# Softmax of three half blocks summed by ScalarE, and a new order of issue, in an attention and feed-forward kernel on one core

## The chip, the cores and the metric

The kernel runs on one core of a Trainium2 chip. The time is the device time of one execution in microseconds (us). Before the change three runs took 591.66, 591.89 and 592.00 us, with a median of 591.89 us. The core has five engines that work beside each other and wait for each other by semaphores: TensorE (PE, matrix products), VectorE (DVE), ScalarE (ACT), GpSimd (POOL) and SyncE (SP, which issues all loads and stores here).

## The reference

The reference computes chunked attention and feeds it to a two-layer network with a gate between the layers:

```python
for c in range(nc):                       # 24 chunks of 32 queries
    k_full = concat([mem_k, k[c_start-16 : c_end+8]])   # 8 + 56 keys
    scores = scale * q_c @ k_full.T       # scale = 1 / sqrt(64)
    scores = scores - max(scores)
    a = exp(scores)
    a = a / (sum(a) + 1e-09)
    out[c] = a @ v_full
h = x @ w_in                              # x: 3072 x 512, w_in: 512 x 2048
g = where(h >= 1, h, where(h <= -1, 0, (h + 1)**2 / 4))
return g @ w_out                          # w_out: 2048 x 512
```

There are 4 batches, 8 heads, 768 positions and 64 numbers a head. All inputs and the output are float32; the two weight matrices come in as 64-bit words.

## The kernel before

**Blocks and halves.** The 3072 tokens are cut into six blocks of 512, and each block into two halves of 256. For a half block PE makes the scores (tile `ps_s`, two PSUM banks of 128 x 1024 numbers in all: 16 groups of 64 keys on 128 partitions), the softmax turns them into probabilities (`pr`), DVE transposes these in 32 x 32 squares (`pt`), PE multiplies them with the values (`ps_x`), and the result is split into a rounded part and a residual (`xth`, `xtl`) for the layers. The first block goes another way: its heads come in four parts (`first_attention`), and PE transposes the probabilities.

**Banks.** The scores and the value products of every half block lie in the same two banks (tag `s`). The next one can't be written before the last reader of the one ahead is done with them. Parts three and four of the first block lie in another pair (tag `a1`).

**Layers.** The hidden width of 2048 is cut into 16 slices. For a slice and a block, PE makes a hidden product of 12 matmuls (rounded weight by rounded x, residual weight by rounded x, rounded weight by residual x; tile `ps_h`), ACT and DVE make the gate (two ACT instructions into `gw`, one DVE minimum, one ACT rounding into `gh`, one DVE residual into `gl`), and PE makes 12 output matmuls (`ps_o`). Products over half a block have 128x256 instead of 128x512 hidden matmuls.

**Weights.** Each pair of weight slices is loaded once and decoded (`decode`): one ACT instruction, two DVE instructions into `f`, one ACT rounding into `wr`, one DVE residual into `wr`.

**Softmax before.** DVE takes the maximum of each group of 64 (`mx`), DVE writes scores less maximum to `pr`, ACT takes the exponent of all 128x1024 in one instruction, DVE sums (`den`), and `divide` adds 1e-9, takes the reciprocal and multiplies. One part of the first block (`SUMMED = (2,)`) already goes another way: there ACT reads the scores' bank group by group, and each instruction gives a group's exponents and its sum.

**Order.** Every engine runs its instructions in the order in which the program issues them (`InOrder`). For the first two blocks and the attention of the third, that order is a table, `FIRST` (line 32): each name in it advances one chain by one step. `L0` to `L39` start a load; `g0` to `g3` are the four parts of the first block's attention; `n0`, `n1` are the two halves of the second block, `n2`, `n3` those of the third; `u0` to `u3` and `w2` to `w15` decode weights; `A`, `B` and `J` are slices of the first block's layers (first half, second half, whole block), and `C`, `D`, `E` those of the second block. `J14` is slice 14 of the first block over the whole block. The last four blocks are issued by the loop at line 662, which isn't touched. The diff's parts stand in `decode` (line 157), `less_max` (338) and `attention` (453); `divide` (211) is called by both ways of the softmax.

Of the kernel before, what the change touches and what calls it, by code (L numbers as in the profile page):

```python
# [29 lines left out]


FIRST = """
    L0 L1 L5 g0 L2 L3 u0 L9 L8 g0 g0 L6 g0 g0 u0 g1 g2 g0 u0 u0 L10 g0 g1 g1 g0 g0 g1 u1 g1 L12 g1
    L7 g1 L4 L13 L11 g1 u2 g0 g1 g2 g1 L14 u2 u0 g0 g1 u2 u1 g2 g3 L16 u1 L15 g2 g0 g2 u2 g2 g3 g1
    L30 u3 u1 L18 g1 g3 g0 L17 u1 L19 g0 g0 g2 g3 g3 g3 A0 g2 A1 g3 g3 A0 A0 u2 g3 w2 g3 g2 A1 L26
    L21 u3 L25 L27 L20 g3 u3 u3 w2 A2 g3 w2 A1 A0 g3 L22 A1 g2 u3 w2 n0 g2 w2 A0 B0 n0 A1 A0 A2 B0
    w3 w4 A1 A2 n0 B0 w3 A3 w4 B1 w3 A2 A3 L28 B0 A3 B0 L23 L31 B0 B2 L24 B1 w3 B1 w4 A2 w3 n0 w5 w5
    L32 L29 B2 B3 B2 B1 B3 A3 A2 n0 n0 B3 A3 w5 w7 w4 B2 J4 B1 B3 J4 n0 w4 B2 n0 n0 J4 B1 J4 n0 w7
    n0 B2 J5 A3 w5 w5 n0 w13 w6 w8 w7 J6 w6 B3 w6 J5 J4 J5 B3 w6 w6 n0 J4 J6 w12 n0 J5 w8 J5 w7 w10  # L39
    J7 J5 w7 J6 w8 J7 w8 w12 J6 n0 w9 w12 w8 J7 n0 w12 J6 J8 J9 J6 J7 J8 w12 n0 w9 J7 w10 w9 n0 J8  # L40
    w9 J8 J9 w11 w9 n1 w10 J9 w11 n1 L33 J10 w10 J7 n1 J8 w10 L34 n1 w11 J10 J10 w15 J10 n1 w13 w14
    J9 J8 J13 n1 w13 J10 n1 J13 J9 J13 n1 n2 J11 w11 J13 w13 J9 J11 w11 J13 w13 J11 n1 w15 n1 J12 n1
    w15 n1 J12 J11 J12 J10 w14 J11 w14 n2 C0 n1 w15 n1 n2 J14 w14 J12 J11 J14 w15 n2 w14 n2 J14 n2
    J12 C0 J14 n1 n2 n2 n2 J12 C0 n2 J15 C1 J14 J15 n1 J13 C1 J15 C0 C0 J15 J15 C1 n1 n1 C2 J14 L36
    J15 n2 C2 C1 L35 J15 n2 J15 n2 n2 C2 J15 C3 C0 C3 C3 C1 n2 C3 n2 D0 D0 D1 D0 C2 D1 D0 J15 D1 D0
    n2 C2 C3 n2 n3 D2 n2 D2 D3 D0 C1 D3 D1 D3 n3 D2 n2 n2 D1 E4 D2 n2 E5 E4 C2 D1 C3 D2 n2 n2 E4 n3
    E4 D3 n3 E4 n3 E5 E5 D3 E5 n3 E7 n3 D2 n3 E5 E7 E7 E6 E8 E6 n3 D3 E4 E7 E5 E6 n3 E6 E6 E9 n3 E8
    n3 E8 E7 E6 E8 E9 n3 n3 E8 E12 L37 E9 E10 E10 E7 E10 E13 n3 E8 E9 L38 L39 E9 E12 E10 n3 E10 E12
    n3 E9 E12 E10 E12 E13 n3 E13 E11 E14 E13 E13 E11 E11 E14 E11 E11 n3 E15 E11 E12 E15 E13 n3 E15
    E14 n3 n3 E14 E15 n3 n3 E14 E15  # L50
"""

LAST = 2
# [1 line left out]

SUMMED = (2,)
HALVED = (0,)
SLICED = (0,1)


class InOrder:
# [13 lines left out]
def attn_ffn_kernel(ctx: ExitStack, tc: tile.TileContext, first_qk, first_v, qk, vw, first_w, w, out):  # L75
    nc = tc.nc
    engines = (nc.tensor, nc.scalar, nc.vector, nc.gpsimd, nc.sync)
    pe, act, dve, pool, sp = (InOrder(tc, e) for e in engines)
# [14 lines left out]
    apool = ctx.enter_context(tc.tile_pool(name="apool", bufs=1))  # L93
# [6 lines left out]
    def two_banks(tag, name):  # L100
        return ps_2.tile([P, 2, 512], F32, name=name, tag=tag)
# [55 lines left out]
    def decode(i, parts=(0, 1)):  # L157

        at = slice(parts[0] * DM, (parts[-1] + 1) * DM)
        pairs = raw[i].rearrange("p (n two) -> p n two", two=2)[:, at]  # L160
        low, u = pairs[:, :, 0], pairs[:, :, 1]
        high = u.bitcast(F32)

        act.activation(high, high, AF.Prelu, scale=2.0**-112, alpha=-(2.0**32))
        yield
        f = apool.tile([P, n2], U32, name="f", bufs=2)[:, at]
        dve.tensor_scalar(f, u, 3, None, op0=ALU.logical_shift_left)
        yield
        dve.scalar_tensor_tensor(f, low, 29, f, op0=ALU.logical_shift_right, op1=ALU.bitwise_or)
        yield  # L170
        f = f.bitcast(F32)
        if i not in ws:
            ws[i] = const.tile([P, 2 * n2], F32R, name=f"wr_{i}", tag=f"w_{i}")
        hi, lo = ws[i][:, 0:n2][:, at], ws[i][:, n2 : 2 * n2][:, at]
        act.copy(hi, f)
        yield
        dve.tensor_tensor(lo, f, hi.bitcast(F32), op=ALU.subtract)
        yield


    scores_of, prob, prob_t, banks, rows_of, turned, xts, both = {}, {}, {}, {}, {}, {}, {}, {}
# [46 lines left out]
    def first_attention(g):  # L228
# [30 lines left out]
        for at in (slice(0, 1), slice(1, 2)) if g in HALVED else (slice(0, 2),):  # L259
# [59 lines left out]
    G = 2 * NP * 2  # L319
# [27 lines left out]
    def transpose_prob(key):

# [104 lines left out]
    def attention(key):  # L453

        pe_scores(key)
        yield
        yield from less_max(key)
        act.activation(prob[key], prob[key], AF.Exp, scale=SCALE)
        yield
        yield from normalise(prob[key])  # L460
        yield from transpose_prob(key)
        if key[0] < first:
            pe_values(key)
            yield
# [12 lines left out]
        yield from split_low(key)
# [184 lines left out]
    for s in range(first * NFC, steps):  # L662
# [5 lines left out]
        if k_values is not None:  # L668
            ps = two_banks("s", "ps_x")
# [28 lines left out]
        else:  # L698
            n, i = LAST // LAG, s - first * NFC
# [22 lines left out]
def _lay_out(q, k, v, mem_k, mem_v, moe_w_in, moe_w_out):  # L722
# [84 lines left out]
```

## Time and profile before

| What | Value |
|---|---|
| Median of three runs | 591.89 us |
| Time of the profiled execution | 591.89 us |
| Span in its profile (first to last instruction) | 590.1 us |
| Granted TensorE clock, mean | 0.998 |
| PE busy | 573.8 us (97%) |
| DVE busy | 338.0 us (57%) |
| ACT busy | 256.9 us (44%) |

The span is 1.8 us shorter than the time. The shares are means over the whole program: DVE is busy 98% in some stretches of the first 110 us, and under a quarter at the end. A matmul's end is modelled, so a busy PE is not always a PE at its full pace; starts of matmuls show the pace.

### The profile page before, as it was taken

Reading aid. Unit: us, or ns where it says so; the run is one execution under the profiler, and the core shown is the slowest. Engines: PE = TensorE matmul, PEld = TensorE weight load, DVE = VectorE, ACT = ScalarE, POOL = GpSimd, SP = SyncE. Lnnn points to the kernel's source line nnn. Section 1 sums busy time; section 2 is a strip of 40 time slices with the busy share of each in tenths; the row PEclk is TensorE's granted clock in tenths of the full one; section 3 lists DMA queues with packets and bytes.
Section 4 is the critical chain, followed back from the end, with each engine's and each line's share of the span. In section 5 each row is a group of like instructions: output and inputs, shape, how many; then the busy total and the mean of one; then the engine's idle time right before and its main releaser. Section 6 shows DMA issues by size and latency. Waiting matters only on the chain.

```text
span 590.1 us, 12015 instructions
## 1 busy us (share of the span) xinstructions
PE 573.8 (97%) x5364; PEld 474.8 (80%) x5364; DVE 338.0 (57%) x497; ACT 256.9 (44%) x430; POOL 2.4 (0%) x7
## 2 busy tenths in 40 slices
PE   4899999999999999999999999999999999999996
PEld 2798888789888888888888888888888888888885
DVE  5899999955643334857624765833684752322222
ACT  3986956344524334343433343333443443433331
POOL 1000000000000000000000000000000000000000
PEclk9999999999999999999999999999999999999999
DMA  8999632205002004103201223201320000100001
GB/s 314 422 418 427 246 111 109 73 37 217 1 1 72 2 0 179 36 38 109 72 1 73 108 72 109 73 1 61 119 72 2 1 1 0 73 1 1 0 1 71
DMA packets 10708, 54.91 MB, mean 93 GB/s; under 512 B 1184, under 2 KB 1184, under 8 KB 6304
## 3 DMA queue, kind: packets, MB, share of 16 engines
q1 hardware_dynamic: 10656, 54.14, 24.1%
q8 instruction: 42, 0.69, 0.5%
q14 instruction: 10, 0.08, 0.0%
HBM read 47.84 MB, written 6.29 MB: 92 GB/s over the span
## 4 chain that ended last, share of the span: by engine, by line
PE 80%; DVE 7%; issue 2%; ACT 2%; DVEq 0%; ACTq 0%
PE ps_o L69 39%; PE ps_h L69 38%; PE ps_x L69 2%; DVE f L69 2%; PE ps_s L69 2%; DVE pt L69 1%; DVE gw L69 1%; DVE gl L69 1%; DVE wr L69 1%; DVE pr L69 0%; DVE den L69 0%; ACT gw L69 0%; DVE mx L69 0%; ACT w L69 0%; ACT wr L69 0%
## 5 line engine op out<-in xcount | busy, mean ns | idle before, releaser
L69 PE MATMUL ps_h<-xth,wr 128*128 128x512 f32 (+1 forms) x832 | 194.5, 376 | 1.1 <-ACT xth L69 1.1
L69 PE MATMUL ps_o<-wr,gh 128*128 128x512 f32 x768 | 194.4, 390 | 0.0
L69 PEld LDWEIGHTS ps_h<-xth,wr 128*128 128x128 f32 x832 | 147.6, 188 | 30.3 <-ACT xth L69 1.3
L69 PEld LDWEIGHTS ps_o<-wr,gh 128*128 128x128 f32 x768 | 143.6, 188 | 29.5
L69 DVE SCALAR_TENSOR_TENSOR gw<-ps_h,gw 128x512 f32<-128x512 f32 (+1 forms) x104 | 67.2, 647 | 140.4 <-ACT gw L69 139.9
L69 ACT ACTIVATE gw<-ps_h 128x512 f32<-128x512 f32 (+1 forms) x104 | 58.5, 563 | 182.5 <-PE ps_h L69 174.1
L69 PE MATMUL ps_o<-wr,gl 128*128 128x512 f32 x384 | 107.1, 390 | 0.5 <-DVE gl L69 0.5
L69 PE MATMUL ps_h<-xtl,wr 128*128 128x512 f32 (+1 forms) x416 | 104.4, 373 | 0.0
L69 DVE TENSOR_TENSOR gl<-gw,gh 128x512 fp32r<-128x512 f32 (+1 forms) x104 | 67.1, 647 | 52.6 <-ACT gh L69 49.9
L69 ACT CAST gh<-gw 128x512 fp32r<-128x512 f32 (+1 forms) x104 | 60.6, 585 | 66.8 <-DVE gw L69 56.6
L69 PEld LDWEIGHTS ps_h<-xtl,wr 128*128 128x128 f32 x416 | 74.9, 188 | 13.9
L69 PEld LDWEIGHTS ps_o<-wr,gl 128*128 128x128 f32 x384 | 71.9, 188 | 16.1 <-DVE gl L69 1.2
L69 ACT ACTIVATE gw<-gw 128x512 f32<-128x512 f32 (+1 forms) x104 | 62.3, 599 | 3.3
L69 DVE STREAM_TRANSPOSE pt<-pr 32x512 f32<-32x512 f32 (+1 forms) x60 | 41.5, 699 | 1.3
L69 DVE STREAM_TRANSPOSE xt<-xr 32x512 f32<-32x512 f32 (+1 forms) x48 | 33.1, 700 | 8.7 <-ACT xr L69 8.0
L69 ACT ACTIVATE pr<-pr 128x1024 f32<-128x1024 f32 (+1 forms) x13 | 12.5, 960 | 30.3 <-DVE pr L69 30.3
L69 PEld LDWEIGHTS ps_s<-qk 64*32 64x32 f32 x1536 | 16.6, 111 | 11.1 <-DMA qk<-in_first_qk_dram 7.2
L69 PE MATMUL ps_s<-qk 64*32 64x64 f32 x1536 | 19.6, 236 | 6.0 <-DMA qk<-in_first_qk_dram 5.1
L69 DVE COPY ob<-ps_o 128x512 f32<-128x512 f32 (+1 forms) x16 | 9.6, 622 | 23.0 <-PE ps_o L69 23.0
L69 ACT ACTIVATE w<-w 128x1024 f32<-128x1024 f32 (+1 forms) x18 | 18.4, 1036 | 6.3 <-DMA w<-in_first_w_dram 6.3
L69 ACT CAST wr<-f 128x1024 fp32r<-128x1024 f32 (+1 forms) x18 | 17.1, 951 | 7.8 <-DVE f L69 7.7
L69 DVE TENSOR_TENSOR wr<-f,wr 128x1024 fp32r<-128x1024 f32 (+1 forms) x18 | 19.7, 1098 | 0.6 <-ACT wr L69 0.5
(36 smaller groups left out, 201.0 us busy)
## 6 DMA issues: line engine op xcount, KB each, us to landing
qk<-in_qk_dram SPq DMA_DIRECT2D x10, 1536.0 KB, 7.1
w<-in_w_dram SPq DMA_DIRECT2D x14, 1024.0 KB, 19.8
v<-in_vw_dram SPq DMA_DIRECT2D x10, 1024.0 KB, 5.0
out_dram<-ob SPq DMA_DIRECT2D x24, 256.0 KB, 2.1
qk<-in_first_qk_dram SPq DMA_DIRECT2D x8, 336.0 KB, 6.9
w<-in_first_w_dram SPq DMA_DIRECT2D x4, 512.0 KB, 8.2
v<-in_first_v_dram SPq DMA_DIRECT2D x4, 512.0 KB, 9.3
```

What stands on the lines that cost most here:

```text
L69: return self.tc.keep_in_program_order(getattr(self.engine, name)(*args, **kwargs))
```

## The change

For the two halves of the second block and the first half of the third, the softmax takes the way of part three of the first block. DVE takes the maximum and multiplies it by minus the scale (a small instruction on 128x16). ACT then reads the scores' banks in 16 instructions on 128x64, each with its group's maximum as bias, and each also gives the sum of its 64 exponents. The subtraction and the sum on DVE fall away for these three, and the exponent in one instruction on ACT. The 16 are issued in four steps of four, so that other work can stand between them. The other halves stay as they were.

`FIRST` is written anew from its first name on. `FLOORED` is empty, so the new branch of `decode` is never taken; `U16` is used only there.

```diff
 FIRST = """
-    L0 L1 L5 g0 L2 L3 u0 L9 L8 g0 g0 L6 g0 g0 u0 g1 g2 g0 u0 u0 L10 g0 g1 g1 g0 g0 g1 u1 g1 L12 g1
...
+    L2 L0 L1 g0 g0 L3 g1 L5 g0 g0 g1 g0 g1 g0 g1 u0 L6 L10 g0 L8 g1 u2 g1 u0 u1 L9 g1 L7 g0 L12 L13
...
-SLICED = (0,1)
+SLICED = (0, 1)
+SUMMED_HALVES = ((1, 0), (1, 1), (2, 0))
+FLOORED = ()
...
-    def less_max(key):
+    def masked(key):
         ps = scores_of.pop(key)
...
         prob[key] = apool.tile([P, G, W], F32, name="pr")
-        yield from softmax_less_max(ps.rearrange("p h (g w) -> p (h g) w", w=W), prob[key])
+        return ps.rearrange("p h (g w) -> p (h g) w", w=W)
+
+    def less_max(key):
+        yield from softmax_less_max(masked(key), prob[key])
+
+    def summed(key):
+
+        s, pr = masked(key), prob[key]
+        mx = apool.tile([P, G], F32, name="mx", bufs=2)
+        dve.tensor_reduce(mx, s, axis=AX.X, op=ALU.max)
+        dve.tensor_scalar_mul(mx, mx, -SCALE)
+        yield
+        den = apool.tile([P, G], F32, name="den", bufs=2)
+        for i in range(G):
+            act.activation(pr[:, i], s[:, i], AF.Exp, bias=mx[:, i : i + 1], scale=SCALE, accum_out=den[:, i : i + 1])
+            if i % 4 == 3:
+                yield
+        yield from divide(pr, den)
...
-        yield from less_max(key)
-        act.activation(prob[key], prob[key], AF.Exp, scale=SCALE)
-        yield
-        yield from normalise(prob[key])
+        if key in SUMMED_HALVES:
+            yield from summed(key)
+        else:
+            yield from less_max(key)
+            act.activation(prob[key], prob[key], AF.Exp, scale=SCALE)
+            yield
+            yield from normalise(prob[key])
```

**The first place: DVE at the start of the program.** `ps_s` are scores of a part of the first block, `pr_...` its probabilities, `w_...` a raw pair of weight slices and `f` its decoded form. Before:

```order
L69 MEMSET ps_s 32x2x2x16
L69 TENSOR_REDUCE mx<-ps_s 128x2x2
L69 TENSOR_TENSOR pr_133<-ps_s,mx 128x2x128
L69 TENSOR_REDUCE mx<-ps_s 128x2x2
L69 TENSOR_TENSOR pr_133<-ps_s,mx 128x2x128
L69 TENSOR_SCALAR f<-w_91 128x512
L69 SCALAR_TENSOR_TENSOR f<-w_91,f 128x512
L69 TENSOR_REDUCE den<-pr_133 128x8
L69 MEMSET ps_s 32x2x2x16
```

With the change:

```order
L72 MEMSET ps_s 32x2x2x16
L72 TENSOR_REDUCE mx<-ps_s 128x2x2
L72 TENSOR_TENSOR pr_126<-ps_s,mx 128x2x128
L72 TENSOR_REDUCE mx<-ps_s 128x2x2
L72 MEMSET ps_s 32x2x2x16
L72 TENSOR_REDUCE mx<-ps_s 128x8
L72 TENSOR_TENSOR pr_126<-ps_s,mx 128x2x128
L72 TENSOR_TENSOR pr_126<-ps_s,mx 128x512
L72 TENSOR_REDUCE den<-pr_126 128x8 x2
```

The second part's softmax moves up into the first's, and the first weights' decoding moves behind both. On SP all four loads for the two parts (`L2 L0 L1 L3`) now stand ahead of the first weights (`L5`), and the load of the second part's first piece stands first.

**The second place: ACT around the exponents of the third block's first half.** `pr` and `den` are its probabilities and sums, the `gw` on 128x512 ahead of them is the gate of `J14`, `wr_1478` is the last but one pair of weights, and `xth` the rounded attention of the second block's second half. Before:

```order
L69 ACTIVATE gw<-ps_h 128x512
L69 ACTIVATE gw<-gw 128x512
L69 ACTIVATE pr<-pr 128x1024
L69 ACTIVATE gw<-ps_h 128x256
L69 ACTIVATE gw<-gw 128x256
```

With the change:

```order
L72 ACTIVATE gw<-ps_h 128x512
L72 ACTIVATE gw<-gw 128x512
L72 ACTIVATE pr,den<-ps_s,mx 128x64 x8
L72 CAST gh<-gw 128x256
L72 CAST wr_1478<-f 128x1024
L72 ACTIVATE pr,den<-ps_s,mx 128x64 x8
L72 CAST gh<-gw 128x512
L72 CAST xth<-ps_x 128x4x2x64 x2
```

One instruction becomes sixteen, with the rounding of a half block's gate and of a pair of weights between them, and the rounding of the attention behind them.

**The third place: PE at the same stretch.** `ps_x` is the value product of the second block's second half, in the banks that held the third block's scores. Before, from the hidden product of `J14` on:

```order
L69 MATMUL ps_h<-xth,wr_1290 128x512 x8
L69 MATMUL ps_h<-xtl,wr_1290 128x512 x4
L69 MATMUL ps_o<-wr_981,gh 128x512 x8
L69 MATMUL ps_o<-wr_981,gl 128x512 x4
L69 MATMUL ps_x<-pt,v 64x32 x64
L69 MATMUL ps_o<-wr_1290,gh 128x512 x8
L69 MATMUL ps_o<-wr_1290,gl 128x512 x4
L69 MATMUL ps_h<-xth,wr_1391 128x512 x8
```

With the change:

```order
L72 MATMUL ps_h<-xth,wr_1361 128x512 x8
L72 MATMUL ps_h<-xtl,wr_1361 128x512 x4
L72 MATMUL ps_h<-xth,wr_205 128x256 x8
L72 MATMUL ps_h<-xtl,wr_205 128x256 x4
L72 MATMUL ps_o<-wr_1121,gh 128x512 x8
L72 MATMUL ps_o<-wr_1121,gl 128x512 x4
L72 MATMUL ps_o<-wr_1361,gh 128x512 x8
L72 MATMUL ps_o<-wr_1361,gl 128x512 x4
L72 MATMUL ps_x<-pt,v 64x32 x64
```

Between the hidden product of `J14` and the value product there was one output product; now there are a half block's hidden product (`C1`) and two output products (`J11`, `J12`).

## Rows read from the trace of the kernel before

**Rows 1.** The page's first lines (the span, and for each engine busy time, share and number of instructions), and the first line of its part on the chain that ended last: shares of the span by engine.

```profile
span 590.1 us, 12015 instructions
PE 573.8 (97%) x5364; PEld 474.8 (80%) x5364; DVE 338.0 (57%) x497; ACT 256.9 (44%) x430; POOL 2.4 (0%) x7
...
PE 80%; DVE 7%; issue 2%; ACT 2%; DVEq 0%; ACTq 0%
```

**Rows 2.** Stretches of the program: start and end, length, busy time of PE, PEld, DVE, ACT and POOL with the number of instructions, granted clock, DMA share, GB/s.

```profile
0.00:10.00 10.00, 4.56 (x132) 2.20 (x132) 3.56 (x9) 2.87 (x4) 2.44 (x7) 1.00 0.78 266
20.00:30.00 10.00, 8.54 (x158) 7.59 (x140) 9.34 (x17) 9.49 (x19) 0.00 (x0) 1.00 1.01 419
...
50.00:60.00 10.00, 10.00 (x45) 8.01 (x44) 9.77 (x13) 6.17 (x8) 0.00 (x0) 1.00 1.03 432
...
100.00:110.00 10.00, 9.98 (x66) 8.24 (x64) 9.81 (x13) 5.79 (x9) 0.00 (x0) 1.00 0.00 0
```

**Rows 3.** PE's waits in the first 220 us: what waited for what, us in total, how often, the longest.

```profile
PE ps_s L69 <- DMA qk<-in_first_qk_dram: 5.1, 4, 2.9
...
PE ps_h L69 <- ACT xth L69: 1.1, 1, 1.1
...
PE ps_o L69 <- DVE gl L69: 0.5, 1, 0.5
```

**Rows 4.** PE in order of time at the start: start us, us, what, how many, and in brackets the idle time ahead and what ended it. The third row is the second part's scores, the fourth the first hidden product (`A0`), the last the scores of the second block.

```profile
3.90 0.68 PE L69 MATMUL ps_s<-qk 64*32 64x64 f32 x32 [0.82 <-DMA qk<-in_first_qk_dram]
4.95 0.68 PE L69 MATMUL ps_s<-qk 64*32 64x64 f32 x32 [0.37 <-DMA qk<-in_first_qk_dram]
8.55 0.68 PE L69 MATMUL ps_s<-qk 64*32 64x64 f32 x32 [2.92 <-DMA qk<-in_first_qk_dram]
...
23.24 1.22 PE L69 MATMUL ps_h<-xth,wr 128*128 128x256 f32 x8 [1.09 <-ACT xth L69]
...
30.94 1.48 PE L69 MATMUL ps_s<-qk 64*32 64x64 f32 x128
```

**Rows 5.** PE in order of time around 114 us, and its last row.

```profile
108.69 1.07 PE L69 MATMUL ps_o<-wr,gl 128*128 128x512 f32 x4
109.77 2.07 PE L69 MATMUL ps_x<-pt,v 64*64 64x32 f32 x128
111.77 2.11 PE L69 MATMUL ps_o<-wr,gh 128*128 128x512 f32 x8
114.40 1.20 PE L69 MATMUL ps_o<-wr,gl 128*128 128x512 f32 x4 [0.51 <-DVE gl L69]
115.43 1.98 PE L69 MATMUL ps_h<-xth,wr 128*128 128x512 f32 x8
...
118.15 1.12 PE L69 MATMUL ps_h<-xth,wr 128*128 128x256 f32 x8
...
119.59 2.00 PE L69 MATMUL ps_o<-wr,gh 128*128 128x512 f32 x8
...
585.21 0.39 PE L69 MATMUL ps_o<-wr,gl 128*128 128x512 f32 x1
```

**Rows 6.** DVE in order of time at the start: the first mask, the two rows with a wait, and the scaling of the third part's maximum.

```profile
5.78 0.11 DVE L69 MEMSET ps_s<- 32x64 f32 x1 [4.64 <-PE ps_s L69]
...
8.40 0.43 DVE L69 TENSOR_SCALAR f<-w 128x512 uint32<-128x512 uint32 x1 [0.80 <-ACT w L69]
...
12.46 0.69 DVE L69 TENSOR_REDUCE den<-pr 128x8 f32<-128x512 f32 x1 [0.38 <-ACT pr L69]
...
15.55 0.17 DVE L69 TENSOR_SCALAR mx<-mx 128x8 f32<-128x8 f32 x1
```

**Rows 7.** Groups of instructions of the whole program by form: engine, operation, out<-in, shapes, how many, busy us in all, mean ns of one, idle time ahead.

```profile
L69 ACT ACTIVATE gw<-gw 128x512 f32<-128x512 f32 x88 | 55.6, 632 | 2.8
...
L69 ACT ACTIVATE gw<-ps_h 128x512 f32<-128x512 f32 x88 | 52.4, 596 | 170.0 <-PE ps_h L69 165.2 <-DVE gl L69 4.7
...
L69 ACT CAST wr<-f 128x1024 fp32r<-128x1024 f32 x14 | 14.7, 1049 | 7.1 <-DVE f L69 7.0
L69 ACT ACTIVATE pr<-pr 128x1024 f32<-128x1024 f32 x10 | 10.6, 1060 | 28.7 <-DVE pr L69 28.7
...
L69 ACT CAST gh<-gw 128x256 fp32r<-128x256 f32 x16 | 6.1, 396 | 2.7 <-DVE gw L69 2.7
...
L69 ACT ACTIVATE pr<-ps_s,mx 128x64 f32<-128x64 f32 x8 | 2.4, 325 | 0.0
...
L69 ACT ACTIVATION_READ_ACCUMULATOR pr<-ps_s,mx 128x1 f32 x8 | 1.7, 218 | 0.0
...
L69 DVE TENSOR_TENSOR pr<-ps_s,mx 128x1024 f32<-128x1024 f32 x10 | 12.2, 1222 | 0.3
L69 DVE TENSOR_REDUCE den<-pr 128x16 f32<-128x1024 f32 x10 | 12.1, 1213 | 0.6 <-ACT pr L69 0.6
```

**Rows 8.** ACT in order of time: the first and second and the end of the eight exponents of part three of the first block, and the rounding that `A0` waits for.

```profile
16.84 0.32 ACT L69 ACTIVATE pr<-ps_s,mx 128x64 f32<-128x64 f32 x1
...
17.15 0.31 ACT L69 ACTIVATE pr<-ps_s,mx 128x64 f32<-128x64 f32 x1
...
19.07 0.24 ACT L69 ACTIVATION_READ_ACCUMULATOR pr<-ps_s,mx 128x1 f32 x1
...
22.60 0.58 ACT L69 CAST xth<-ps_x 128x512 fp32r<-128x512 f32 x1
```

More of the change, by code (lines that the diff above doesn't have):

```diff
@@ L12 @@
 U32 = mybir.dt.uint32
+U16 = mybir.dt.uint16
 AF = mybir.ActivationFunctionType
@@ L32 @@
 FIRST = """
-    L0 L1 L5 g0 L2 L3 u0 L9 L8 g0 g0 L6 g0 g0 u0 g1 g2 g0 u0 u0 L10 g0 g1 g1 g0 g0 g1 u1 g1 L12 g1
[L34 to L47, printed above, removed]
@@ L48 @@
-    n3 E8 E7 E6 E8 E9 n3 n3 E8 E12 L37 E9 E10 E10 E7 E10 E13 n3 E8 E9 L38 L39 E9 E12 E10 n3 E10 E12
-    n3 E9 E12 E10 E12 E13 n3 E13 E11 E14 E13 E13 E11 E11 E14 E11 E11 n3 E15 E11 E12 E15 E13 n3 E15
-    E14 n3 n3 E14 E15 n3 n3 E14 E15
+    L2 L0 L1 g0 g0 L3 g1 L5 g0 g0 g1 g0 g1 g0 g1 u0 L6 L10 g0 L8 g1 u2 g1 u0 u1 L9 g1 L7 g0 L12 L13
+    g1 g1 u0 u0 g0 u2 L4 g0 g2 u2 g0 g1 L16 u2 g2 g1 g2 u0 u2 L14 L15 u1 g2 g3 L11 L30 g2 g0 L20 g1
+    g2 g3 g3 g0 g2 L17 g3 g1 g3 g3 g0 g0 g3 g3 A0 g2 w2 g3 u1 A0 g3 w2 A0 L19 u1 g2 u1 g3 u3 g3 g2
@@ new lines @@
+    A1 A2 w2 u3 g2 g3 L18 u3 L21 A1 n0 w2 A1 u3 A0 B0 L23 w2 A0 L29 L22 A2 L26 A2 w6 u3 L27 A1 B0 A1
+    L25 L31 A2 L28 L32 w3 w3 B0 A2 A3 A3 A0 A3 A1 B0 w5 B1 L24 A3 w3 B1 w3 B2 B0 B2 n0 w4 B1 B2 w5
+    B1 n0 B0 n0 B2 w3 B1 w4 w5 B3 B3 n0 B2 B3 w4 A3 w5 n0 J4 J4 w4 w15 n0 w5 n0 w6 B3 w6 w7 A2 B1 w6
+    w12 w8 w4 J4 B2 B3 n0 J6 w6 n0 J4 w8 n0 A3 J5 B3 J5 w9 n0 J5 J4 J4 w7 J5 n0 J5 J7 w7 n0 n0 w8
+    w13 J6 w7 n0 w7 w8 n0 J6 n0 w12 w12 J6 J7 J7 J6 w10 n0 J5 J8 w8 J8 n1 J9 w11 w9 n1 J8 J6 n1 w12
@@ new lines @@
+    w12 n1 w10 J13 L34 J7 J8 J8 w10 w10 n1 J7 w9 w10 w9 n1 J9 J13 L33 w9 J7 n1 w11 w13 J9 J8 J10 w11
+    J13 n1 n2 w11 J9 J9 w11 n1 J12 J13 J10 J10 J10 J10 w13 n1 n1 J9 J11 n1 J12 J12 J13 w15 n2 J12
+    w13 J10 J11 J11 J12 n1 w14 w13 C0 J14 n1 w14 C0 J11 J11 C0 J14 C1 J11 n1 n2 n2 w14 C0 J12 w15
+    J14 w14 n2 n2 n1 n2 J14 n1 C1 w14 n2 J14 n2 C1 n2 J15 J13 C2 J15 n1 J15 J15 C1 w15 C0 n2 L35 L36
+    n2 w15 C1 J15 C3 J14 n2 n1 C3 C3 D0 J15 C3 C2 D0 D0 n2 n2 C2 J15 D1 n2 D2 J15 D0 D1 C2 D1 C2 n2
@@ L51 @@
+    C0 D3 C1 n2 n2 C3 D2 D1 J15 n2 D2 D1 n3 D3 n2 n2 D0 D3 J15 E4 D0 D3 E4 n2 E4 D1 C2 E4 n2 D2 D2
+    n2 E5 D2 E6 E4 D3 E5 C3 E5 n3 D3 E7 n3 E5 E6 E5 E6 E4 E9 E5 E6 E7 n3 n3 E7 L37 E7 E7 E6 E8 E8 E8
+    E9 n3 E8 E8 n3 E9 E6 E10 E7 E12 E10 E10 E9 n3 n3 E9 E10 E8 E12 E10 E12 E9 E11 E12 E11 n3 E11 n3
+    E11 n3 E11 n3 E12 n3 E13 E10 E14 E13 E13 n3 E13 E14 n3 E15 E13 n3 E11 E15 n3 n3 n3 E15 E14 L38
+    E12 n3 E14 E15 n3 L39 n3 E13 n3 E15 E14
 """
@@ L166, in decode @@
         f = apool.tile([P, n2], U32, name="f", bufs=2)[:, at]
-        dve.tensor_scalar(f, u, 3, None, op0=ALU.logical_shift_left)
-        yield
-        dve.scalar_tensor_tensor(f, low, 29, f, op0=ALU.logical_shift_right, op1=ALU.bitwise_or)
-        yield
+        if i in FLOORED:
+            upper = raw[i].bitcast(U16).rearrange("p (n four) -> p n four", four=4)[:, at, 1]
+            act.activation(f, upper, AF.Copy, bias=2.0**-14 - 0.5, scale=2.0**-13)
+            yield
+            dve.scalar_tensor_tensor(f, u, 3, f, op0=ALU.logical_shift_left, op1=ALU.bitwise_or)
+            yield
+        else:
+            dve.tensor_scalar(f, u, 3, None, op0=ALU.logical_shift_left)
+            yield
+            dve.scalar_tensor_tensor(f, low, 29, f, op0=ALU.logical_shift_right, op1=ALU.bitwise_or)
+            yield
         f = f.bitcast(F32)
@@ L344, in less_max @@
         prob[key] = apool.tile([P, G, W], F32, name="pr")
-        yield from softmax_less_max(ps.rearrange("p h (g w) -> p (h g) w", w=W), prob[key])
+        return ps.rearrange("p h (g w) -> p (h g) w", w=W)
[6 more added lines that the diff above has]
+        dve.tensor_scalar_mul(mx, mx, -SCALE)
+        yield
+        den = apool.tile([P, G], F32, name="den", bufs=2)
+        for i in range(G):
+            act.activation(pr[:, i], s[:, i], AF.Exp, bias=mx[:, i : i + 1], scale=SCALE, accum_out=den[:, i : i + 1])
+            if i % 4 == 3:
+                yield
+        yield from divide(pr, den)
     def transpose_prob(key):
@@ L456, in attention @@
         yield
-        yield from less_max(key)
-        act.activation(prob[key], prob[key], AF.Exp, scale=SCALE)
-        yield
-        yield from normalise(prob[key])
+        if key in SUMMED_HALVES:
+            yield from summed(key)
+        else:
+            yield from less_max(key)
+            act.activation(prob[key], prob[key], AF.Exp, scale=SCALE)
+            yield
+            yield from normalise(prob[key])
         yield from transpose_prob(key)
```

## Prediction

> **What bounds the kernel now.** I read the page first, then the table of stretches, then PE's waits, then PE, DVE and ACT in order of time where waits stand. The page has PE busy for 97% of the span, and PE makes 80% of the chain that ended last [rows 1]. The reader is to see that this is not the whole story: DVE is nearly full in the first 110 us (9.3 to 9.8 of 10 us in the stretches shown), and ACT is at 9.5 of 10 around 25 us and about 6 later [rows 2]. So one could think that work taken from DVE is time gained. The starts of PE's groups say no. From 23.24 us, where the first hidden product begins [rows 4], PE's groups follow each other at a steady pace: 12 matmuls on 128x512 take 2.72 us (115.43 to 118.15), 12 on 128x256 take 1.44 (118.15 to 119.59) [rows 5]. After 23.24 PE waits once for more than 0.2 us, for a residual of DVE's at 114 us (0.5 by the profile's count [rows 3, 5]). The group ahead of it runs from 111.77 to 114.40, 2.63 us where 1.81 is usual (2.72 less the 0.91 of its last four); so the wait costs 0.8. One group earlier, 108.69 to 109.77 is 1.08 where 0.91 is usual: the value product there waits 0.17 for the scores' banks. All else that PE loses lies ahead of 23.24, for loads (5.1 us), ACT and DVE [rows 3]. The last matmul starts at 585.21 [rows 5], and copies and stores make up the rest to 590.1 [rows 1].
>
> So the end moves only by (a) when PE gets going, (b) the 1.0 us around 110 to 114, and (c) new waits of PE's.
>
> **DVE and ACT, the softmax itself.** For each of the three halves, DVE loses a subtraction (1222 ns) and a sum (1213), about 2.3 us by pace, and gains a scaling of 128x16 of some 0.17 (the 128x8 one [rows 6]). That is 2.1 us each, 6.4 in all. ACT loses one exponent (1060) and gains 16 on 128x64 [rows 7]. The rows name 325 ns and 218 ns for reading the sum, but they overlap: starts are 0.29 apart (16.84 to 17.15 with its neighbours, eight from 16.84 to the end at 19.31 [rows 8]). 16 at 0.29 are 4.7 us, 3.6 more than before, 11 in all.
>
> The Trainium skill's page "ScalarE: Activation LUTs", section "What ACT_TABLE_LOAD costs", has an ACTIVATE with a bias per partition at about 280 ns plus 0.833 ns a number, less 93 where they follow each other: 240 ns for 64 numbers, an estimate of 3.8 us for 16. The trace has 4.7, as each one is followed by a row for its sum. By the page's figure the wait worked out under (c) for the banks would be gone and the sum 0.3 lower.
>
> DVE's 6.4 us are worth no more than what PE waits for DVE, which is (b): as two of the three halves, 4.2 us, lie ahead of 114 us, the residual comes well before PE asks for it. ACT's 11 us are hidden as long as PE has other products in its order; where not, they are (c).
>
> **(a) The start.** The four loads of the first two parts come first now. The first part needs the second and third of them. The first two landed 1.05 us apart (3.90 and 4.95 [rows 4]), so I take the third at 6.0 and the fourth at 7.05, and DVE's first mask at 6.83 instead of 5.78 [rows 6]. The second part's scores, at 8.55 before [rows 4], are some 1.5 us earlier. From there DVE no longer waits: before, the stretch from 5.78 to 15.72 (end of the scaling of the third part's maximum) took 9.94 us, of which 0.80 and 0.38 were waits for ACT [rows 6], leaving 8.76. The new order has one more weight step pair ahead of this point (0.43 [rows 6] and about 0.6, half of the 1222 that a two-operand row on 128x1024 takes [rows 7]), so 9.8 at most; as two softmaxes now alternate, a row less often waits for its predecessor, and I take 9.5. The scaling ends at 16.3, ACT's eight exponents begin at 16.35 instead of 16.84: 0.5 earlier. From there to `A0` were 6.40 us (16.84 to 23.24), made of the exponents, two copies, the fourth part's maximum and subtraction and the rounding of `xth` that ended at 23.18 [rows 8]. In the new order the fourth part's exponent (about 0.6, a little over half of the 1060 on 128x1024 [rows 7]) stands ahead of that rounding and two weight steps behind it, and I keep 6.4. `A0` starts at 22.75.
>
> Between `A0` and the second block's scores stands the same work in another order: `A0`, the fourth part's transposes and two value products, `A1`, `A2`. Before, `A1` and `A2` covered the fourth part's softmax. Now its transposes come right behind `A0` (a wait of some 0.3 for DVE's multiplication) and its value product behind two copies of ACT's that stand behind a weight step and a gate (some 0.5). These 0.3 more than eat what was won: before there were small waits of 0.2 there. So the second block's scores start at 30.9 again: (a) is 0, with bounds of -0.7 (the copies come in time) and +0.7 (the third load lands a us later, as the loads behind 4.95 did).
>
> **(b)** -1.0 us: 0.8 and 0.17.
>
> **(c) New waits.** The surest is at the third block's scores. Its banks are read by ACT until the 16th exponent, and the value product of the second block's second half is written there next. From the end of `J14`'s hidden product ACT has the gate (596 and 632, about 1.24), eight exponents (2.33), a rounding of 128x256 (about 0.31 at pace, 396 as a row), a rounding of weights (about 0.95; 1049) and eight more (2.33) [rows 7, 8]: 7.16 us. PE has `C1` (1.44), `J11` and `J12` (2.72 each): 6.88 [rows 5]. PE waits 0.3. For the second block's halves, a chunk of four exponents (1.16) stands ahead of a rounding of weights in several places, and DVE then waits for the rounding and PE for DVE's residual. Where I follow it along the order, PE is 0.1 late at the first half's value product and about 0.3 at `J8`'s output product, which needs the residual of its weights. No row of before shows such a wait; its bounds are 0 (PE's products cover it) and one chunk at each of these two places, 2.3. I take 0.4, near the lower end, as DVE has 2 us less to do per half. (c) is +0.7.
>
> The loop from the third block's layers on, and the tail, are unchanged: before, PE ran there without a gap, and the third block's second half still has four groups of 2.72 us between its value product and the loop.
>
> **Sum.** 0 - 1.0 + 0.7 = -0.3 us on the profiled execution's 591.89 (which is the median, too): 591.6. What two runs can tell apart here is about 0.2%, 1.2 us; the forecast is no change.
>
> **Rivals.**
> 1. *Both gains are kept.* PE gets going 0.5 to 0.7 earlier, the wait at 114 goes (-1.0), and the new waits stay out, since DVE's lead of 4 us covers them: 591.89 - 0.6 - 1.0 = 590.3, down to 590.0. For it speaks that DVE is the fuller engine (9.8 of 10 [rows 2]); against it that ACT's chain in front of the second block's scores is as full (9.5 of 10 [rows 2]).
> 2. *ACT takes DVE's place (slower).* ACT runs in order, and what stands behind a chunk, a weight rounding or a gate, is asked for by DVE and PE. If PE waits a chunk for each of the three halves, 3 x 1.16 = 3.5, less the 1.0 of (b): 594.4; it is slower by over 1.2 us from 2.2 us of new waits on. For it: between 40 and 110 us ACT goes from 6 to about 7 of 10. Against it: PE has two to four products between a hidden product and its output product.
> 3. *The start is late.* The third load lands a us later and the first softmaxes with it: +0.7 - 1.0 + 0.7 = +0.4, 592.3. This is still no change.
>
> **How the numbers follow.** The forecast with rival 3: 0.62. Rival 1: 0.21. Rival 2: 0.17. The likeliest case's own range is 590.8 to 592.8. For 8 in 10 the range reaches to half of rival 1 and the near end of rival 2: 590.2 to 593.4. Faster by over 0.2% (under 590.7): 0.21; within: 0.63; slower (over 593.1): 0.16.
>
> **What would show it.** `A0` starting between 22.5 and 23 us and the second block's scores near 30.9 would confirm (a). PE's wait for a residual near 114 us gone, and DVE with waits for ACT's weight roundings between 70 and 115 us, would confirm (b) and the cost on ACT. A PE wait of about 0.3 for ACT ahead of the value product near 114 would confirm (c). I am wrong if the second block's scores start before 30.2 or after 31.6, or if PE's waits between 35 and 120 us add up to over 2 us, or if they are none.

## The result, and the profile after

The changed kernel takes 595.53 us (median of six runs, 594.94 to 595.76), the kernel before 591.80 us beside it. The ratio is 1.0064, 95% interval 1.0054 to 1.0075: 3.7 us slower. The forecast was 591.6, no change, with a range from 590.2 to 593.4.

The page of the changed kernel, as [rows 1]:

```profile
span 593.7 us, 12105 instructions
...
PE 575.3 (97%) x5364; PEld 474.6 (80%) x5364; DVE 331.5 (56%) x494; ACT 268.5 (45%) x523; POOL 2.4 (0%) x7
...
PE 80%; DVE 1%; ACT 1%; issue 0%; DVEq 0%; ACTq 0%
```

DVE has 6.5 us less to do and ACT 11.6 more, close to what was worked out (6.4 and 11). The span is 3.6 us longer all the same. The stretches, as [rows 2], show where the engines lost their fullness:

```profile
20.00:30.00 10.00, 8.21 (x151) 7.16 (x133) 8.46 (x16) 8.38 (x15) 0.00 (x0) 1.00 1.02 422
50.00:60.00 10.00, 9.44 (x41) 7.19 (x40) 9.25 (x13) 9.48 (x17) 0.00 (x0) 1.00 1.02 431
100.00:110.00 10.00, 10.00 (x52) 8.43 (x51) 9.49 (x15) 5.10 (x9) 0.00 (x0) 1.00 0.00 0
```

From 50 to 60 us ACT was busy 6.17 us before and is now at 9.48, and PE has fallen from 10.00 to 9.44. PE's waits in the first 220 us, as [rows 3], now hold entries that were not there:

```profile
PE ps_s L72 <- DMA qk<-in_first_qk_dram: 2.9, 2, 1.5
...
PE ps_h L72 <- ACT xth L72: 0.9, 1, 0.9
...
PE ps_o L72 <- ACT wr L72: 0.6, 1, 0.6
PE ps_o L72 <- DVE wr L72: 0.6, 1, 0.6
PE ps_x L72 <- DVE pt L72: 0.4, 1, 0.4
PE ps_h L72 <- DVE gw L72: 0.3, 1, 0.3
PE ps_x L72 <- ACT pr L72: 0.2, 1, 0.2
```

The old `DVE gl` wait is gone. PE in order of time at the start, as [rows 4] (first part's scores, two loads later the rest, `A0`, the second block's scores):

```profile
4.50 0.68 PE L72 MATMUL ps_s<-qk 64*32 64x64 f32 x32 [1.42 <-DMA qk<-in_first_qk_dram]
6.66 1.63 PE L72 MATMUL ps_s<-qk 64*32 64x64 f32 x96 [1.48 <-DMA qk<-in_first_qk_dram]
...
23.04 1.22 PE L72 MATMUL ps_h<-xth,wr 128*128 128x256 f32 x8 [0.91 <-ACT xth L72]
...
31.36 1.48 PE L72 MATMUL ps_s<-qk 64*32 64x64 f32 x128
```

And around 114 us, as [rows 5] (the third row is an output product of the whole block, the last the value product of the second block's second half):

```profile
109.72 1.08 PE L72 MATMUL ps_h<-xtl,wr 128*128 128x512 f32 x4
111.07 1.22 PE L72 MATMUL ps_h<-xth,wr 128*128 128x256 f32 x8 [0.26 <-DVE gw L72]
...
112.61 2.00 PE L72 MATMUL ps_o<-wr,gh 128*128 128x512 f32 x8
114.45 1.07 PE L72 MATMUL ps_o<-wr,gl 128*128 128x512 f32 x4
115.36 1.98 PE L72 MATMUL ps_o<-wr,gh 128*128 128x512 f32 x8
...
118.43 2.07 PE L72 MATMUL ps_x<-pt,v 64*64 64x32 f32 x128 [0.19 <-ACT pr L72]
```

By starts (the distance from one start to the next, less the same distance where nothing waits), PE loses 0.27 us at a hidden product at 51, 0.73 at an output product at 55, 0.27 at one at 60, 0.67 at the first half's value product (66.13 to 68.80, 2.00 usual), 0.21 ahead of the second half's scores, 1.22 at an output product at 88, 0.44 at 111 and 0.35 at the value product at 118: 4.2 in all. With the start 0.42 later and the 1.0 of (b) won, this makes the 3.6.

DVE's waits of the changed kernel between 24 and 92 us, in order of time, say more than PE's:

```profile
27.83 0.69 DVE L72 TENSOR_TENSOR wr<-f,wr 128x512 fp32r<-128x512 f32 x1 [1.28 <-ACT wr L72]
...
36.89 0.69 DVE L72 TENSOR_SCALAR f<-w 128x1024 uint32<-128x1024 uint32 x1 [1.61 <-ACT w L72]
42.66 0.43 DVE L72 SCALAR_TENSOR_TENSOR gw<-ps_h,gw 128x256 f32<-128x256 f32 x1 [0.61 <-ACT gw L72]
...
50.72 0.17 DVE L72 TENSOR_SCALAR den<-den 128x16 f32<-128x16 f32 x1 [1.42 <-ACT pr L72]
...
80.52 1.23 DVE L72 TENSOR_TENSOR wr<-f,wr 128x1024 fp32r<-128x1024 f32 x1 [1.77 <-ACT wr L72]
```

With five smaller ones these waits add up to 8.2 us. In the kernel before there are three, 0.8 in all:

```profile
32.11 1.23 DVE L69 TENSOR_TENSOR wr<-f,wr 128x1024 fp32r<-128x1024 f32 x1 [0.15 <-ACT wr L69]
...
40.57 0.42 DVE L69 SCALAR_TENSOR_TENSOR gw<-ps_h,gw 128x256 f32<-128x256 f32 x1 [0.31 <-ACT gw L69]
...
72.16 1.22 DVE L69 TENSOR_TENSOR wr<-f,wr 128x1024 fp32r<-128x1024 f32 x1 [0.38 <-ACT wr L69]
```

DVE was given 4.2 us in this stretch (two halves) and idles 7.3 more.

Three theories followed. Theory 1: the 16 exponents a half are too much for ACT's queue. Theory 2: the new order of issue costs the time by itself. Theory 3, made after the first runs: PE follows DVE through the first 115 us, so each wait of DVE's for ACT is lost for good, whoever put it there.

### The profile page after: what moved, and what is told of

Its sections match the earlier page's. It is cut to its first block, busy times and chain, and to the rows that moved or that the text cites. A ratio compares the mean times of both kernels' runs of the same rounds, so it can differ in the third digit from the quotient of the medians.

```text
span 593.7 us, 12105 instructions
## 1 busy us (share of the span) xinstructions
PE 575.3 (97%) x5364; PEld 474.6 (80%) x5364; DVE 331.5 (56%) x494; ACT 268.5 (45%) x523; POOL 2.4 (0%) x7
## 4 chain that ended last, share of the span: by engine, by line
PE 80%; DVE 1%; ACT 1%; issue 0%; DVEq 0%; ACTq 0%
PE ps_o L72 38%; PE ps_h L72 38%; PE ps_x L72 2%; PE ps_s L72 2%; ACT pr L72 0%; DVE wr L72 0%; ACT wr L72 0%; DVE pt L72 0%; DVE f L72 0%; DVE ob L72 0%; DVE gl L72 0%; ACT gh L72 0%; ACT ob L72 0%; DVE gw L72 0%; DVEq L833 0%
## 5 line engine op out<-in xcount | busy, mean ns | idle before, releaser
L72 ACT ACTIVATE pr<-pr 128x1024 f32<-128x1024 f32 (+1 forms) x10 | 9.3, 930 | 33.9 <-DVE pr L72 33.9
L72 DVE SCALAR_TENSOR_TENSOR f<-w,f 128x1024 uint32<-128x1024 uint32 (+1 forms) x18 | 19.7, 1100 | 0.1
```

The source lines that it names most:

```text
L72: return self.tc.keep_in_program_order(getattr(self.engine, name)(*args, **kwargs))
```

## The experiments

Times are medians; each run of a kernel stands beside runs of the kernel before on the same chip (591.5 to 591.7 us), and "+" is the difference to those. Of the table, a diff shows only the names around a step that moves.

**Order and softmax apart.** In the first two kernels only one part of the change is made.

```diff
-SUMMED_HALVES = ((1, 0), (1, 1), (2, 0))
+SUMMED_HALVES = ()
```

The steps of `n0`, `n1` and `n2` that fall away are taken out of the table. 

> The new order, but all three halves keep the softmax of before (subtraction and sum on DVE, one exponent of 128x1024 on ACT). Theory 1 (the 16 exponents per half stand in ACT's queue ahead of weight roundings and gates; they cost PE about 4 us between 45 and 120 us): ACT loses 3.6 us of work per half, the waits of DVE's weight residuals and of den for ACT go; the start stays 0.4 late; DVE has 2.1 us more per half, so up to 1.5 us of PE's waits for DVE come instead: 591 to 593.5 us. Theory 2 (the new order of loads, weights and gates costs the time, whatever the softmax is): 594.5 to 596, with PE's waits at the same places as in the changed kernel.

Measured: 595.22 us, +3.6 (ratio 1.0060, 1.0047 to 1.0072). With ACT's load as before, nothing is won: theory 1 can't hold alone. Where DVE's relief went stands in its rows. Here is DVE of this kernel (no exponents to wait for, but a subtraction and a sum more):

```profile
36.68 0.69 DVE L72 TENSOR_SCALAR f<-w 128x1024 uint32<-128x1024 uint32 x1 [1.62 <-ACT w L72]
...
50.96 0.17 DVE L72 TENSOR_SCALAR den<-den 128x16 f32<-128x16 f32 x1
51.04 1.22 DVE L72 TENSOR_TENSOR wr<-f,wr 128x1024 fp32r<-128x1024 f32 x1
```

At `den` DVE is at 50.96, and in the changed kernel at 50.72. Of the 2.1 us that the first half gave to DVE most went into the wait for its exponents (1.42). The waits at 27.83 and 36.89 are here too (1.28, and 1.62 at 36.68): they come from the new order, not from the exponents.

The other part alone is the table of before with the `SUMMED_HALVES` of the change; of the four steps with exponents the last two stand one behind the other. 

> The order of before, but the three halves are summed by ACT; each fourth step of exponents follows right behind the third. Theory 1: the start is as before (the second block's scores at 30.9), but ACT's 11 us more stand in its queue between 45 and 120 us: 594 to 597 us. Theory 2: DVE's 6.4 us less and the order of before together give 590.5 to 592.5 us.

Measured: 604.40 us, +12.8 (1.0217, 1.0203 to 1.0231). Worse than theory 1 said. PE in order of time, and two stretches (columns as [rows 2]):

```profile
111.75 1.07 PE L72 MATMUL ps_o<-wr,gl 128*128 128x512 f32 x4
119.68 3.64 PE L72 MATMUL ps_x<-pt,v 64*64 64x32 f32 x128 [6.86 <-ACT pr L72]
123.24 3.63 PE L72 MATMUL ps_o<-wr,gh 128*128 128x512 f32 x8
```

```profile
112.00:116.00 4.00, 0.82 (x4) 0.36 (x2) 2.60 (x3) 3.79 (x13) 0.00 (x0) 1.00 0.00 0
...
120.00:124.00 4.00, 4.00 (x127) 3.84 (x123) 2.44 (x4) 1.31 (x3) 0.00 (x0) 0.50 0.02 4
```

In the old order the value product of the second half comes when the third block's first exponents have only begun, and PE waits 6.86 us for the banks, until the last of them is read. Then the granted clock is 0.50 (1.2 GHz), and the value product takes 3.64 us instead of 2.07. In the new order, with three products set ahead of it, this wait is 0.19 (118.43 above).

**One half back.** `SUMMED_HALVES = ((1, 1), (2, 0))`. 

> The changed kernel, with the softmax of before for the second block's first half alone. Theory 1: the losses between 45 and 67 us (0.3 at a hidden product at 51 us, 0.7 at the output product at 55, 0.3 at the one at 60, 0.5 at the first half's value product: 1.8 in all) go, the others stay: 593.5 to 594 us. Theory 2: no change, 595 to 596, or later by DVE's 2.1 us.

Measured: 595.92 us, +4.3 (1.0069, 1.0057 to 1.0082). A miss for theory 1: without the first half's exponents the loss up to 67 us stays.

`SUMMED_HALVES = ((1, 0),)`. 

> The changed kernel, with the softmax of before for the second block's second half and the third block's first half; only the second block's first half is summed by ACT. Theory 1: the losses between 74 and 120 us (0.25 ahead of the second half's scores, 1.2 at an output product at 88, 0.4 at a hidden product at 111, 0.35 at the second half's value product: 2.2 in all) go, those up to 67 us stay, and up to 1 us of the wait for DVE near 114 us may come back: 593.2 to 594.5 us. Theory 2: no change, 595 to 596.

Measured: 594.59 us, +3.0 (1.0047, 1.0035 to 1.0060). It lies between the two. Of the second half's losses little goes: from its scores to the third block's PE takes 19.1 us, and 19.3 in the changed kernel.

**Single waits of DVE's.** No work is changed in the next four; steps change places in the table.

```diff
-    w15 n0 w5 n0 w6
+    w15 w5 n0 n0 w6
```

> The changed kernel; the only edit is that the small addition to the sums of the second block's first half (den) stands behind the residual of the sixth weights (w5) on DVE instead of ahead of it. Theory 3 (DVE is what PE waits for between 50 and 90 us; in the new order it idles, waiting for ACT, and each such wait is a loss that stays): of the 1.42 us that DVE waits for the exponents, some 1.2 go, DVE is 1.2 earlier from 51 us on, PE's waits up to 67 us shrink by about as much: 594.2 to 594.8 us. Theories 1 and 2 (ACT's total, or the new order of PE and the loads): neither is touched, 595 to 596.

Measured: 594.41 us, +2.8 (1.0053, 1.0041 to 1.0066): 1.0 less than the changed kernel's +3.7, and inside theory 3's range. Two of the five runs (595.33 and 595.52) lie among the changed kernel's, though, and part of the gain in the profile is an early start. The second block's scores stand at 31.36 in the changed kernel and here at

```profile
30.44 1.48 PE L72 MATMUL ps_s<-qk 64*32 64x64 f32 x128
```

From there to the third block's scores PE takes 61.97 us here and 62.65 in the changed kernel: the move itself is worth 0.7, for 1.0 us of idle time that DVE has less.

```diff
-    n1 w12
-    w12 n1 w10
+    w12 n1
+    w12 n1 w10
```

> The changed kernel; the only edit is that ACT's rounding of the weights w12 stands ahead of the first four exponents of the second block's second half, where ACT idles 1.36 us, instead of behind them. Theory 3: DVE's wait of 1.77 us for that rounding at 80.5 us goes, and with it most of PE's 1.2 us at the output product at 88: 594.0 to 594.8 us. Theories 1 and 2: 595 to 596.

Measured: 594.19 us, +2.5 (1.0047, 1.0034 to 1.0060): 1.2 less. The wait of 1.77 is gone, and with it PE's wait at 88; from the second block's scores to the third's PE takes 61.67 us, 1.0 less. The next wait of DVE's, for a gate's rounding behind the exponents, grew from 0.28 to 1.17.

```diff
-    A2 w6 u3
+    A2 u3
...
-    A3 A3 A0
+    A3 A3 w6 A0
```

> The changed kernel; the only edit is that ACT's first step on the weights w6 stands some 3 us later, behind that on w3, which DVE needs first. Theory 3: DVE's wait of 1.61 us at 36.9 us shrinks by about 1.05; by 0.5 to 1.0 of it PE is earlier at 67 us, if the wait for the exponents at 50.7 us does not take it back: 594.5 to 595.5 us. Theories 1 and 2: 595 to 596.

Measured: 594.91 us, +3.3 (1.0055, 1.0041 to 1.0069). A miss of the edit: DVE's wait did not shrink. The time lies in theory 3's range all the same, but by the start: from the second block's scores to the end of the profiled execution there are 564.13 us, and 564.17 in the changed kernel.

```profile
36.29 0.69 DVE L72 TENSOR_SCALAR f<-w 128x1024 uint32<-128x1024 uint32 x1 [1.83 <-ACT w L72]
```

Ahead of `w3`'s step on ACT stands a gate that waits for PE; with `w6`'s step gone from in front of it, ACT idled there instead. The step has to go ahead of that gate.

All three together: 

> The changed kernel with all three moves (w6's first step later, den's addition behind w5's residual, w12's rounding ahead of the exponents); no work is added or taken away. Theory 3: 1.05, 1.2 and 1.77 us of DVE's idle time go, and PE's waits between 45 and 90 us with them: 591.5 to 593.0 us. Theory 1 (ACT's total) and theory 2 (what the new order does to PE's own order and the loads): 595 to 596.

Measured: 593.70 us, +2.0 (1.0036, 1.0023 to 1.0049). Clearly better than the changed kernel with the same work on each engine, but short of theory 3's number, as one of the three does nothing.

**Ten moves.** Four places of them:

```diff
-    L27 A1 B0 A1
-    L25 L31 A2 L28 L32 w3 w3 B0
+    L27 A1 w3 B0 A1
+    L25 L31 A2 L28 L32 w3 B0
...
-    w7 n0 n0 w8
+    n0 n0 w7 w8
...
-    w12 n1 w10 J13 L34 J7 J8 J8
+    w12 J7 J8 n1 w10 J13 L34 J8
...
-    J14 w14 n2 n2
+    J14 n2 n2 w14
```

> The changed kernel with ten steps moved by a few places each and no work added or taken away: w3's first ACT step ahead of the first gate of B0 and w6's behind it; den's addition and w12's rounding as in the run with three moves; ACT's roundings of J7's and J8's gates ahead of the second four exponents of the second half; DVE's second step on w7 behind the first half's last transposes; J4's residual, C0's gate minimum and the second residual of the first half's attention one or two places earlier; w14's rounding behind the third block's exponents. Theory 3 (what is lost is DVE's idle time in waits for ACT, and PE's waits that follow from it; neither ACT's total nor the new order as a whole): PE's waits between 43 and 120 us, 2.5 us in the run with three moves, nearly all go: 590.8 to 592.3 us. Theories 1 and 2: about 593.7, as with three moves, or more.

Measured: 592.00 us, +0.5 (1.0007, 0.9998 to 1.0016). Inside theory 3's range. Some of the ten change DVE's own order (`J4`'s residual, `C0`'s minimum, the attention's second residual, the step on `w7`); what each of them gave was not taken apart.

One step more:

```diff
-    n0 w12 w12 J6 J7 J7 n0 J6
+    n0 n0 w12 w12 J6 J7 J7 J6
```

> The kernel with ten moves, in which the second residual of the first half's attention on DVE stands right behind the first one, not only ahead of J6's residual: the second half's scores waited 0.67 us there, until that residual had read their banks. Theory 3: that wait goes, and the start alone (0.3 to 0.4 late) is left of the changed kernel's loss, against the 1.0 us won near 114 us: 590.8 to 591.6 us. Rival: the scores wait for something else there (their load): 592.0 again.

Measured: 591.81 us, +0.3 (1.0003, 0.9995 to 1.0012); the time is 0.2 above theory 3's range and not told apart from the run ahead, but the wait is gone in PE's rows (hidden, scores), where the scores follow at the usual 1.00:

```profile
70.89 1.07 PE L72 MATMUL ps_h<-xtl,wr 128*128 128x512 f32 x4
71.89 1.48 PE L72 MATMUL ps_s<-qk 64*32 64x64 f32 x128
```

**What the softmax is worth there.** The same table with `SUMMED_HALVES = ()`: 

> The moved order of the run ahead, but with the softmax of before in all three halves, so DVE has 6.4 us more to do and ACT 11 less. Against the moved order with the new softmax (591.8) it tells what the new softmax itself is worth where no wait for ACT hides it. If DVE's relief of 4.2 us ahead of 114 us counts there: 593.5 to 595. If only the waits that the new order made counted, and the relief is worth nothing: 591.3 to 592.3.

Measured: 594.40 us, +2.8 (1.0044, 1.0030 to 1.0058). So DVE's relief is real: 2.6 us. With the new softmax DVE has 4.2 us less to do and idles 1.6 more (5.7 against 4.1 in the table below), which leaves the same 2.6.

**One half in the old order.** ACT had 2.6 us idle ahead of the second half's exponent. The table of before, `SUMMED_HALVES = ((1, 1),)`, exponents in two groups of eight:

```diff
-    n1 J8 w10 L34 n1 w11 J10 J10 w15 J10 n1 w13 w14 J9
+    n1 n1 J8 w10 L34 w11 J10 n1 n1 J10 J10 w13 J9
```

> The order of before, in which only the second block's second half is summed by ACT; its exponents stand in two groups of eight in ACT's queue where ACT idled 2.6 us, den's addition stands next to the reciprocal, and the first steps of w14 and w15 stand a few places later. Theory 3 (DVE's relief is worth what PE waits for DVE, if DVE doesn't wait for the exponents): DVE has 2.1 us less and waits less than 1 us for ACT; the wait for DVE near 114 us and the small one at the value product ahead of it go: 590.5 to 591.0 us. Theory 1 (the 16 exponents on ACT cost PE time wherever they stand): 592 or more. Theory 2 (only the new order costs): 590.5 to 591.7 us.

Measured: 591.93 us, +0.5 (1.0005, 0.9996 to 1.0014). A miss for the expectation: DVE waited 0.89, 0.32, 0.47 and 0.68 us for ACT, and was at 98.19 us at the second half's first transpose, 98.16 before. The wait near 114 us stayed at 0.51.

```diff
-    J7 n1 n1 J8 w10 L34 w11 J10 n1 n1 J10 J10 w13 J9
+    J7 J10 n1 n1 n1 n1 J8 w10 L34 w11 J10 J10 J9 w13
```

> The order of before with the second block's second half summed by ACT, placed anew: J10's gate, whose matmuls end at 81.8 us, stands ahead of the 16 exponents on ACT and not between them, w11's and w13's roundings stand around J13's gate, and the first steps of w15 and w14 behind them; on DVE the product with the reciprocal stands ahead of J13's minimum. In the run ahead of this one DVE waited 2.4 us for ACT at four places and so gave its 2.1 us back. Theory 3: those waits shrink to about 1 us, DVE is 1 to 2 us earlier at 98 us and PE's wait for DVE near 114 us goes: 590.4 to 591.0 us. Rival (the wait at 114 us has another cause than DVE's place): 591.5 to 592.

Measured: 591.25 us, -0.3 (0.9992, 0.9983 to 1.0001), not told apart from the kernel before. Half way: one wait of 1.89 us stayed, since `J10`'s gate waits for a buffer that `J8`'s residual frees.

```diff
-    w11 n1 L33 J10 w10 J7 J10 n1 n1 n1 n1 J8
+    J8 w11 n1 L33 J10 w10 J7 J10 J10 n1 n1 J9 J10 n1 n1
```

> As the run ahead with the order of before and one half summed, but J8's residual stands ahead of the maximum on DVE (J10's gate had to wait 2.19 us on ACT until that residual had freed its buffer, and pushed the exponents back), J10's minimum right behind the maximum, and the roundings of J9's and J10's gates between the first eight exponents and the second. If DVE's idle time decides: the wait of 1.89 us for J10's rounding shrinks to under 0.5, DVE is 1.5 to 2 us earlier than before at 98 us, and all of the 1.0 us near 114 us goes: 590.4 to 590.9 us. If half of it is all there is to win: 591.2 again.

Measured: 590.73 us, -0.9 (0.9985, 0.9976 to 0.9994): faster than both kernels. DVE's transpose and PE's output product near 114 us:

```profile
96.75 0.70 DVE L72 STREAM_TRANSPOSE pt<-pr 128x512 f32<-128x512 f32 x1
```

```profile
111.80 2.11 PE L72 MATMUL ps_o<-wr,gh 128*128 128x512 f32 x8
113.75 1.07 PE L72 MATMUL ps_o<-wr,gl 128*128 128x512 f32 x4
114.65 1.98 PE L72 MATMUL ps_h<-xth,wr 128*128 128x512 f32 x8
```

DVE is 1.4 us earlier than before, and 111.80 to 113.75 has no wait in it, against 111.77 to 114.40 [rows 5].

**All runs in one table.** DVE's idle time is the sum of the waits marked in its rows from 24 to 92 us; the last column takes off the 0.8 of the kernel before and 2.1 us for each half of the second block that ACT sums (column "Halves").

| Kernel | Halves | DVE idle | Idle less relief | Time to before |
|---|---|---|---|---|
| changed kernel | 2 | 8.2 | 3.1 | +3.7 |
| new order, old softmax | 0 | 4.7 | 3.8 | +3.6 |
| first half back | 1 | 6.8 | 3.8 | +4.3 |
| first half only | 1 | 6.0 | 3.1 | +3.0 |
| `den` moved | 2 | 7.2 | 2.1 | +2.8 |
| `w12` moved | 2 | 7.1 | 2.1 | +2.5 |
| `w6` moved | 2 | 8.2 | 3.2 | +3.3 |
| three moved | 2 | 7.3 | 2.3 | +2.0 |
| ten moved | 2 | 5.7 | 0.7 | +0.5 |
| ten, one further | 2 | 5.7 | 0.7 | +0.3 |
| the same, old softmax | 0 | 4.1 | 3.2 | +2.8 |
| old order, one half | 1 | 2.5 | -0.4 | +0.5 |
| placed anew | 1 | 2.7 | -0.2 | -0.3 |
| placed anew, again | 1 | 1.3 | -1.6 | -0.9 |
| old order, three halves | 2 | 5.7 | 0.6 | +12.8 |

The last two columns lie within 0.9 us of each other in all kernels but the last. There 3.1 us are lost ahead of the output product at 111.75 (108.69 before), since a long wait of DVE's for the exponents stands just behind the stretch:

```profile
93.14 0.18 DVE L72 TENSOR_SCALAR den<-den 128x16 f32<-128x16 f32 x1 [2.61 <-ACT pr L72]
```

The rest is the wait at 119.68 and the lower clock behind it. The stretch was chosen after the runs; taken to 100 us, the columns lie within 1.3. So this is a reckoning and not a proof of its own (some of DVE's small waits are for work that waits for PE). The proof is in the runs with moved steps: same instructions on each engine, 3.4 us apart, and 3.65 from the second block's scores to the end of the profiled executions (564.17 and 560.52), so the start has no part in it.

## Why the prediction was wrong

**"DVE's 6.4 us are worth no more than what PE waits for DVE, which is (b)."** As the price of relief in the old order this held: at most 1.0 us, and 0.9 measured with one half summed and its steps placed anew. But it was the whole account of DVE. It was read from a kernel in which DVE, busy 9.3 to 9.8 of 10 us [rows 2], still came in time for PE; what a us of new idle time on DVE costs was in no term. Where one wait was taken out, about 1.0 us of idle time was worth 0.7 us (`den`) and 1.0 (`w12`). In the new order, where DVE was late, relief was worth 2.6 us.

**(c), the second block's halves, +0.4.** This is the step that failed: the term of DVE's and PE's new waits for ACT. Measured 3.4 (the places from 51 to 88 us). I looked at two places where a chunk of exponents stands ahead of a weight rounding, bounded them by 2.3 and took the low end "as DVE has 2 us less to do per half". Neither ACT's rows nor the order of DVE's were followed from 24 us on; the waits at 27.83 and 36.89, ahead of the first new exponent, come from the order alone and were in no term, and neither was the 0.44 at 111 us, for a gate's minimum on DVE. So even the upper ends of (a) to (c) together did not reach the result.

**(c), the third block's scores, +0.3.** Right: PE waits for ACT there, 0.35 by starts.

**(b), -1.0.** Right, or 0.1 too large: the last four matmuls ahead of a value product take 1.00 where nothing waits (66.32 to 67.32 in the kernel before), so the 1.08 held a wait of 0.1, not of 0.17. Neither the wait for the residual nor the 0.17 at the value product is left; what stands at 118.43 is the term of (c).

**(a), 0.** Right within its bounds, but not its path. The third load's scores began at 6.66, not at 6.0. DVE's first mask stood at 7.48, not at 6.83. DVE then took 9.2 us from the first mask to the third part's scaling where I took 9.5, and ACT's exponents began at 16.81 (16.35 forecast; 16.84 before). `A0` began at 23.04, just outside the stated 22.5 to 23. The second block's scores, at 31.36 in this profile, were between 30.4 and 31.4 in the ten other kernels with this start, as the first loads land, and between 30.7 and 31.1 in the five with the old one: hardly a loss that stays.

**The softmax's own cost.** Right: 11.6 us more on ACT, 6.5 less on DVE. The first half's 16 exponents begin at 43.88, 47.27 and 49.38 us, and the steps behind them begin at 46.21, 48.44 and 50.54: 4.7 us, as forecast. The Trainium skill's page "ScalarE: Activation LUTs", section "What ACT_TABLE_LOAD costs", by whose figures 16 were an estimate of 3.8 us, is short here too; the trace decides.

**The rivals.** Rival 2 named the outcome (594.4, slower) and the sign of its mechanism, with a chance of 0.17: ACT takes DVE's place. But it priced a chunk for each half in ACT's queue, and the kernel without any exponents of the new kind lost as much. What happened is wider: the new order lets DVE wait for ACT, by gates, weight steps and exponents alike. The statement that PE's waits between 35 and 120 us over 2 us would show the forecast wrong was met: they are 4.2 by starts.

**What stays open.** Which of the waits at 27.83 and 42.66 can be had back was not tried; the best of the moved tables keeps 5.7 us of DVE's idle time.

## What to carry to other kernels

Where two engines are both nearly full and hand work to each other in program order, sum the waits between those two in the new order before pricing the work that moves: relief is worth only what the next engine waits for it, while a new wait on the fuller engine cost 0.7 and 1.0 us for each us of it where one was taken out here. Ask of each wait added which instruction behind it was ready; putting that one first adds no work, and gave back about 0.7 us at one place here. A change of work and a new order belong in separate runs, since each alone (+12.8 and +3.6) told more than both together (+3.7).

## What the runs showed of the hardware

After PE had idled for 6.86 us in the old order with three summed halves, the granted clock was 0.50 from 120 to 124 us, the lower of its two levels (1.2 GHz), and a product that takes 2.07 us took 3.64: the wait cost 6.86 us and some 3 more in the two products behind it.
